# Retention and two feed-forward nets: the first two tiles' feature order, their first order of work, and the last copy

## The chip, the cores and the metric

The kernel runs on one core of one Trainium2 chip. The metric is the device time of an execution in microseconds; the median of the runs is compared. Engines: PE (TensorE, matrix products), DVE (VectorE), ACT (ScalarE), POOL (GpSimd) and SP (SyncE, which here only issues DMAs).

## The reference, cut to what matters

```python
# retention: B, H, S, D = 4, 8, 768, 64;  gamma per head
for t in range(S):
    state = gamma * state + outer(k[t], v[t])
    y[t] = q[t] @ state / sqrt(D)
x = y, as (3072 tokens, 512 features)
h = x @ w_in                                  # 512 x 2048
g = where(h >= 1, h, where(h <= -1, 0, (h + 1)**2 / 4))
x = g @ w_out                                 # 2048 x 512
out = ((x @ w1) * (x @ w2)) @ w3 @ w_out2     # 512 x 1024 twice, 1024 x 1024, 1024 x 512
```

## The kernel before, in words

The 768 steps are cut into six chunks of 128; chunk number c of all four batches makes token tile c with 512 tokens (B x C). Within a chunk retention is three products. "q" or "Q" words (function `scores`, line 507) make the 128 x 128 scores of each head from q and k; DVE multiplies them with a decay mask (line 520). "p" and "P" words (function `values`, line 562 in tiles 0 and 1, line 576 in tiles 2 to 5) make the output from the masked scores and v ("own" products) and, from tile 1 on, add the decayed queries times the state of the chunks before ("state queries", the operand `sbd`). "k" words (line 545) make keys times values, from which ACT and DVE make the next state. The output stands in PSUM, a tile of two banks, features on the partitions. `split_x` takes it out for tiles 0 and 1: ACT rounds it into xh (line 618), DVE takes the rest into xl (line 619); each product in full precision is made of three of such halves (lines 299 to 301). "h" words (tile 0) and "H" words (tile 1), function `plan_h`, are x @ w_in for one of 16 parts of 128 columns, 12 matmuls of 512 columns each; ACT (lines 658, 660) and DVE (line 661) make g of it.

The order of the 512 features differs: in tiles 0 and 1 partition 64h + d of block p holds feature d of head 2p + h; in tiles 2 to 5 the output of head 2p + h lies at partition half e, bank h, block j with p = j + 2e. So w_in's rows are needed in two orders. It is loaded from HBM in the first one by `load_win` (line 371), one DMA of 128 partitions for every 1024 words (pairs of 32-bit words, since the input is kept in its wide form), and converted to 32 bit by two ACT and four DVE operations (lines 332 to 345), then split into halves (lines 355, 357). For tiles 2 to 5 the converted w_in goes to a scratch tensor win_d and comes back in the second order by `load_permuted` (line 701): for each of eight units two DMAs of 64 partitions.

The order of PE's work at the start is written out in FIRST (line 43), where a digit is the batch (q, Q, p, P), the tile (k) or the part of w_in (h, H). A planner gives every other operation a due time from its consumers, loads among them, and a greedy emission writes all instruction streams; for PE it may take an operation from the next twelve if that can start sooner. PSUM has three tiles ("pe") for the scores, values and key products of tiles 0 and 1, and two banks for h and H. POOL scales the keys of tile 0, DVE those of tile 1 and the queries of tile 1 (line 536), once ACT has scaled the decay.

Behind that follow the products with w_out (y words; the chunks of tiles 2 to 5 run beside them), the first net for tiles 2 to 5 in pairs with seven instead of eight block products (`plan_hu`), the fold of w3 with w_out2, and the second net in the same way. The last tile's last 128 rows are copied out by `plan_out` in two halves, columns 0 to 255 by DVE with a DMA from SP, columns 256 to 511 by ACT with a DMA from ACT's queue (lines 931, 933, 1094).

Of the kernel before, what the change touches and what calls it, by code (L numbers as in the profile page):

```python
# [10 lines left out]
U32 = mybir.dt.uint32  # L11
# [5 lines left out]
C = 128  # L17
# [7 lines left out]
NP = H // 2  # L25
# [9 lines left out]
LEAD = 6.0  # L35
# [5 lines left out]
STAY = 8  # L41
MASKED = 6.8
FIRST = """
q0 q3 q2 q1 p2 p1 p3 p0 Q0 h0 Q2 Q1 h1 k0 P1 P2 Q3 P0 h2 P3 h3 H0 H1 H2 k1
h4 h5 H3 h6 h7 h8 H4 H5 H6 h9 H7 H8 h10 h11 h12 H9 h13 h14 H10 h15 H11 H12 H13 H14 H15
"""
KEYS = ("POOL", 1.2), ("DVE", 0.7), ("POOL", 1.2)
RATE = 360.0
# [202 lines left out]
def retention_then_two_ffns(  # L251
# [17 lines left out]
    nc = tc.nc  # L269
# [42 lines left out]
    def new_r(name):  # L312
        return work.tile([P, TT], F32, tag="r", name=name, bufs=3)

    plan = Plan({
# [3 lines left out]
    })  # L319
# [44 lines left out]
    win_d = [dram.tile([P, 1024], F32, name=f"win_d{n}") for n in range(NF1 // 2)]  # L364
    win_kept = {}

    def load_win(f, n):
        src = w_in[f // 2].bitcast(U32)
        c0 = f % 2 * 1024
        def fn(raw, j):  # L370
            nc.sync.dma_start(out=raw[:, 1024 * j:1024 * j + 1024], in_=src[:, c0 + 1024 * j:c0 + 1024 * j + 1024])
        return [(0.43, lambda raw, j=j: fn(raw, j)) for j in range(n)]

    def load_rows(*srcs):
        def one(j, src):
# [94 lines left out]
    def chunk(b, c):  # L470
# [42 lines left out]
        if c < 2:  # L513
            a = half(c, "a")
            a_at = lambda: a.ap.rearrange("p h (a t) -> p h a t", a=NP)
        else:
            a = Val("a", lambda: att.tile([P, 2, NP, C], F32, tag="a", name="a", bufs=1))
            a_at = lambda: a.ap
        if c < 2:
            plan.op("DVE", 1.25, lambda: nc.vector.tensor_tensor(  # L520
                out=a_at().rearrange("p h a t -> p (h a) t"),
# [3 lines left out]
        else:  # L525
            for h in range(2):
                plan.op("DVE", 0.7, lambda h=h: nc.vector.tensor_tensor(
                    out=a_at()[:, h], in0=ps_at(h).rearrange("p (a t) -> p a t", a=NP),
# [6 lines left out]
        if c:  # L535
            scaled_q = [plan.op(eng, many, lambda: ve.tensor_tensor(
                out=q_at(), in0=q_at(), in1=decay, op=ALU.mult), r=[decays], use=[q_], after=[qk, lq])]
# [13 lines left out]
        ps2 = new_ps(c)  # L551
        merged = c >= 2 and not last
        old = sbd.get(b)

        def values():
            q_t, v_t, a_t = q_at(), v_at(), a_at()
            if c < 2:
                for own in (True, False) if c else (True,):
                    for p in range(NP):
                        for h in range(2):  # L560
                            r = slice(64 * h, 64 * h + 64)
                            nc.tensor.matmul(
                                out=ps2.ap[64 * h:64 * h + 64, 0, p * C:(p + 1) * C],
                                lhsT=v_t[:, 2 * p + h, :] if own else old.ap[r, p, :],
                                rhs=a_t[:, h, p, :] if own else q_t[r, p, :],
                                start=p == 0 and own, stop=own == (c == 0), skip_group_check=True,
                            )
                return
            if merged:
                keys_values(ps2.ap[:, 0, 2 * C:2 * C + NP * D], True)  # L570
            for own in (True, False):
                for j in range(NP // 2):
                    for h in range(2):
                        for e in range(2):
                            p, r = j + 2 * e, slice(64 * h, 64 * h + 64)
                            nc.tensor.matmul(  # L576
                                out=ps2.ap[64 * e:64 * e + 64, h, j * C:(j + 1) * C],
                                lhsT=v_t[:, 2 * p + h, :] if own else old.ap[r, p, :],
                                rhs=a_t[:, h, p, :] if own else q_t[r, p, :],
                                start=own and j == 0 and not (merged and h == 0), stop=not own,  # L580
                                skip_group_check=True,
                            )

        pv_ops[b, c] = plan.op(
            "PE", 0.95 + (0.0, 0.86, 0.43)[min(c, 2)] + (0.43 if merged else 0.0), values,
            r=[a, old] if c else [a], w=[ps2], use=[v_, *([q_] if c else []), *([k_] if merged else [])],
            after=[lv, *scaled_q, *(scaled_k if merged else [])],
        )
# [1 line left out]
        if c >= 2:  # L590
            for kb in range(2):
                if (c, kb) not in xs:
                    xs[c, kb] = Val("w", lambda: wpool.tile([P, 2, 512], F32, tag="w", name="xs"))
                plan.op("ACT", 0.45, lambda kb=kb: nc.scalar.copy(
                    out=xs[c, kb].ap[:, :, b * C:b * C + C], in_=got()[:, :, kb]), r=[ps2], part=[xs[c, kb]])
        else:
            split_x(b, c, ps2, lambda: ps2.ap[:, 0, :].rearrange("p (a t) -> p a t", a=NP))

        def update(kv, at):

# [13 lines left out]

    def split_x(b, c, ps2, got):
        xh, xl = x_tile(c)
        view = lambda x: x.ap[:, :, b * C:b * C + C]
        hi = plan.op("ACT", 0.6, lambda: nc.scalar.copy(out=view(xh), in_=got()), r=[ps2], part=[xh])
        plan.op("DVE", 0.7, lambda: nc.vector.tensor_tensor(
            out=view(xl), in0=got(), in1=view(xh), op=ALU.subtract), r=[ps2], part=[xl], use=[xh], after=[hi])  # L620
# [66 lines left out]
    def keep_win(f, after):  # L687
# [5 lines left out]
            r=[w], w=[t], after=after)  # L693
        plan.op("POOL", 0.6, lambda: nc.gpsimd.dma_start(
            out=win_d[f // 2][:, 512 * (f % 2):512 * (f % 2) + 512], in_=t.ap), r=[t], w=[d], size=256)

    def load_permuted(u, n):

        of = win_d[n].rearrange("(h d) (i e w) -> e d i h w", h=2, i=2, e=2)
        for e in range(2):  # L700
            plan.op("SP", 0.45, lambda e=e: nc.sync.dma_start(
                out=u.ap[64 * e:64 * e + 64].rearrange("d (i h w) -> d i h w", i=2, h=2), in_=of[e]),
                r=[win_kept[2 * n], win_kept[2 * n + 1]], part=[u], size=400).lead = LEAD

    def load_whole(u, src, after):
        plan.op("SP", 0.45, lambda: nc.sync.dma_start(out=u.ap, in_=src), w=[u], size=512, after=after).lead = LEAD
# [101 lines left out]
    def plan_hu(i, n):  # L808
        if i < PAIR:
            u = Val("u", lambda: cpool.tile([P, 1024], F32, tag="u", name="u"))  # L810
            load_permuted(u, n)
            uh, ul = plan_unit(u)
            store_unit(n, (uh, ul))
        else:
            uh, ul = load_unit(n)
# [26 lines left out]
        def gate(f, src, src_at, second):  # L842
# [19 lines left out]
            out=c1.ap, in0=pair.ap[:, 0], in1=c1.ap, op=ALU.add), r=[pair], w=[c1])  # L862
# [9 lines left out]
            out=c2.ap, in0=pair.ap[:, 1], in1=c2.ap, op=ALU.add), r=[pair], w=[c2])  # L872
        gate(2 * n, c2, lambda: c2.ap, True)
        plan.op("DVE", 0.7, lambda: nc.vector.tensor_tensor(
            out=c3.ap, in0=c3.ap, in1=c5.ap, op=ALU.add), r=[c5], w=[c3])
# [193 lines left out]
    def plan_out(i, n, f, t):  # L1069

        p, w = pq[i, f, n], wc[f]
        if f == 0:
            evacs[i, n, t] = Val("acc", lambda: psum["acc"].tile([P, DM], F32, tag="acc", name="oacc"))
        ps = evacs[i, n, t]

        def fn():
            lh, ll = (p.ap[:, s, t * P:(t + 1) * P] for s in range(2))
            wh, wl = w.ap[:, 0, :], w.ap[:, 1, :]
            nc.tensor.matmul(out=ps.ap, lhsT=lh, rhs=wh, start=(f == 0), stop=False)  # L1079
            nc.tensor.matmul(out=ps.ap, lhsT=lh, rhs=wl, start=False, stop=False)  # L1080
            nc.tensor.matmul(out=ps.ap, lhsT=ll, rhs=wh, start=False, stop=(f == NF2 - 1))  # L1081

        out_ops[i, n, f, t] = plan.op("PE", 0.681, fn, r=[p, w], w=[ps])
        if f < NF2 - 1:
            return
        r0 = t * S + (2 * i + n) * C
        parts = [(t % 2, nc.sync, 0, 512)]
        if 2 * i + n == NTILE - 1 and t == 3:
            parts = [(0, nc.sync, 0, 256), (1, nc.scalar, 256, 512)]
        for eng, queue, c0, c1 in parts:  # L1090
            st = Val("st", lambda: new_st("ost"))
            plan.op("ACT" if eng else "DVE", 0.63, lambda eng=eng, c0=c0, c1=c1, st=st: evacuate(
                st.ap[:, c0:c1], ps.ap[:, c0:c1], eng), r=[ps], w=[st])
            plan.op("ACT" if queue is nc.scalar else "SP", 0.43, lambda queue=queue, c0=c0, c1=c1, st=st: queue.dma_start(
                out=out[r0:r0 + P, c0:c1], in_=st.ap[:, c0:c1]), r=[st], size=(c1 - c0) / 2).store = True

    with tc.manual_schedule():


        rows, zeros, ones, part = (  # L1100
            wpool.tile([P, 2, 512], F32, tag="w", name=name) for name in ("rows", "zeros", "ones", "part"))
        nc.sync.dma_start(out=small, in_=c_small)
        nc.vector.memset(rows[:, 0], 0.0)
        for h in range(2):
            r = slice(64 * h, 64 * h + 1)
# [6 lines left out]
        for h in range(2):  # L1112
            nc.vector.tensor_tensor(
                out=by_half(part, h), in0=causal.rearrange("p (o t) -> p o t", o=1).to_broadcast([P, NP, C]),
# [3 lines left out]
        for h in range(2):  # L1118
            ps = psum["e"].tile([P, 2, 512], F32, tag="pa", name="begin_ps")
            for n in range(BEGIN * (1 - h)):  # L1120
                nc.tensor.matmul(
                    out=ps[:, 1, 0:P], lhsT=zeros[:, 0, 0:P], rhs=zeros[:, 0, 0:P], start=True, stop=True)
            nc.tensor.matmul(
                out=ps[:, 0], lhsT=ones[:, 0, P * h:P * h + P], rhs=rows[:, 0], start=True, stop=True)
# [53 lines left out]
        qk, pv, kv, h = qk_ops, pv_ops, kv_ops, h_ops  # L1178
# [172 lines left out]
```

## Time and profile before

| | us |
|---|---|
| three runs: median (lowest to highest) | 997.19 (995.87 to 998.01) |
| the profiled execution, its own time | 994.71 |
| its span in the trace | 992.9 |
| PE busy in the span | 984.2 |
| DVE / ACT / POOL busy | 707.5 / 550.8 / 67.2 |

The span is what the trace covers of the profiled execution; the 1.8 us up to its own time lie around it. A page part gives busy shares in 40 slices of the span; the views by stretch give the same for chosen stretches; the timelines give single instructions (or merged runs of the same kind) with their start, their length and, in brackets, what the engine waited for just before. Matmul records overlap, since the engine is pipelined: what a block of them costs is read from start to start.

### The profile page before, as it was taken

What the parts mean: (1) busy time and instruction counts of PE and PEld (TensorE: products, weight loads), DVE (VectorE), ACT (ScalarE), POOL (GpSimd) and SP (SyncE); (2) the same over time, 40 slices, a digit from 0 to 9 for tenths busy, and PEclk for the clock granted to TensorE, in tenths of its full rate; (3) what the DMA queues carried; (4) which work ended last, traced back from release to release, by engine and by line L of the source; (5) the groups of instructions that cost most, each with busy time, mean ns of one, the idle gap of its engine ahead of it and who ended that gap; (6) DMA issues with size and microseconds to landing.
All of it is one profiled execution on the core that took longest, in us unless ns stands there. A gap on an engine that the chain in (4) does not pass through costs nothing.

```text
span 992.9 us, 15259 instructions
## 1 busy us (share of the span) xinstructions
PE 984.2 (99%) x5792; PEld 810.1 (82%) x5792; DVE 707.5 (71%) x1098; ACT 550.8 (55%) x971; POOL 67.2 (7%) x78
## 2 busy tenths in 40 slices
PE   8999999999999999999999999999999999999998
PEld 6888888878888888888888888888888888888886
DVE  8889888566577778776766788577874787657750
ACT  3778866343677767576766564444543446244430
POOL 1121244331000000000000000000000000000000
PEclk9999999999999999999999999999999999999999
DMA  9788899899988769899876971113131130301001
GB/s 326 290 275 307 295 354 382 306 336 360 352 273 284 277 220 403 325 340 341 322 284 252 391 285 68 43 43 106 54 115 40 47 117 33 117 32 43 22 21 65
DMA packets 71421, 212.10 MB, mean 214 GB/s; under 512 B 8370, under 2 KB 12850, under 8 KB 67380
## 3 DMA queue, kind: packets, MB, share of 16 engines
q1 hardware_dynamic: 66816, 195.79, 55.8%
q0 software_dynamic: 4384, 15.21, 3.9%
q8 instruction: 45, 0.74, 0.3%
q14 instruction: 28, 0.23, 0.1%
q10 hardware_dynamic: 148, 0.14, 0.0%
HBM read 154.48 MB, written 56.62 MB: 213 GB/s over the span
## 4 chain that ended last, share of the span: by engine, by line
PE 96%; DMA 2%; DVE 0%; ACT 0%; issue 0%; ACTq 0%; DVEq 0%
PE bank_a L1032 13%; PE y1acc L299 11%; PE y1acc L301 10%; PE y1acc L300 10%; PE bank L828 9%; PE bank_b L1032 7%; PE banks L828 7%; PE oacc L1080 4%; PE oacc L1081 4%; PE oacc L1079 4%; PE bank_c L1032 3%; PE hps L299 3%; PE hps L300 2%; PE hps L301 2%; PE pa L576 2%; PE qk_ps L507 1%
## 5 line engine op out<-in xcount | busy, mean ns | idle before, releaser
L299 PE MATMUL y1acc<-g,wo 128*128 128x512 f32 x384 | 151.4, 394 | 0.0
L301 PE MATMUL y1acc<-g,wo 128*128 128x512 f32 x384 | 149.7, 390 | 0.0
L300 PE MATMUL y1acc<-g,wo 128*128 128x512 f32 x384 | 149.6, 390 | 0.0
L1032 PE MATMUL bank_a<-yop,unit 128*128 128x512 f32 x576 | 145.7, 389 | 0.0
L1032 PEld LDWEIGHTS bank_a<-yop,unit 128*128 128x128 f32 x576 | 108.1, 188 | 22.5
L828 PE MATMUL bank<-xop,unit 128*128 128x512 f32 x384 | 95.3, 389 | 0.0
L299 PEld LDWEIGHTS y1acc<-g,wo 128*128 128x128 f32 x384 | 72.1, 188 | 17.7 <-issue 2.8
L301 PEld LDWEIGHTS y1acc<-g,wo 128*128 128x128 f32 x384 | 72.1, 188 | 15.5 <-DVE g L357 0.4
L828 PEld LDWEIGHTS bank<-xop,unit 128*128 128x128 f32 x384 | 72.0, 188 | 15.1 <-issue 0.2
L300 PEld LDWEIGHTS y1acc<-g,wo 128*128 128x128 f32 x384 | 72.1, 188 | 14.5
L1079 PE MATMUL oacc<-wc,p 128*128 128x512 f32 x192 | 74.7, 389 | 0.0
L1080 PE MATMUL oacc<-wc,p 128*128 128x512 f32 x192 | 74.7, 389 | 0.0
L1081 PE MATMUL oacc<-wc,p 128*128 128x512 f32 x192 | 74.7, 389 | 0.0
L1040 ACT COPY c<-bank_a 128x512 f32<-128x512 f32 x72 | 42.3, 588 | 56.0 <-PE bank_a L1032 55.5
L1032 PE MATMUL bank_b<-yop,unit 128*128 128x512 f32 x288 | 73.1, 389 | 0.0
L828 PE MATMUL banks<-xop,unit 128*128 128x512 f32 x288 | 73.1, 389 | 0.0
L1043 DVE TENSOR_TENSOR c<-c,c 128x512 f32<-128x512 f32 x48 | 33.2, 691 | 51.4 <-ACT c L1040 50.7
L715 ACT CAST unit<-unit_w 128x512 fp32r<-128x512 f32 x96 | 52.0, 565 | 30.0 <-DVE unit_w L723 25.5
L828 PEld LDWEIGHTS banks<-xop,unit 128*128 128x128 f32 x288 | 54.1, 188 | 11.2
L1032 PEld LDWEIGHTS bank_b<-yop,unit 128*128 128x128 f32 x288 | 54.1, 188 | 11.2
L717 DVE TENSOR_TENSOR unit<-unit_w,unit 128x512 fp32r<-128x512 f32 x96 | 57.5, 620 | 6.8 <-ACT unit L715 5.4
L355 ACT CAST p<-c 128x512 fp32r<-128x512 f32 x48 | 29.8, 621 | 48.0 <-DVE c L1043 48.0
(171 smaller groups left out, 1836.5 us busy)
## 6 DMA issues: line engine op xcount, KB each, us to landing
wo<-wo_d SPq DMA_DIRECT2D x80, 512.0 KB, 6.6
unit_w<-sp_wab SPq DMA_DIRECT2D x24, 512.0 KB, 3.3
raw<-in_w_in_dram SPq DMA_DIRECT2D x16, 512.0 KB, 6.6
wo_d<-wo POOLq DMA_DIRECT2D x16, 512.0 KB, 7.0
uh_d<-unit SPq DMA_DIRECT2D x8, 1024.0 KB, 4.7
raw<-in_w_dram SPq DMA_DIRECT2D x16, 512.0 KB, 7.8
unit<-uh_d SPq DMA_DIRECT2D x8, 1024.0 KB, 8.1
raw<-in_w3t_dram SPq DMA_DIRECT2D x8, 1024.0 KB, 6.7
```

What stands on the lines that cost most here:

```text
L299: nc.tensor.matmul(out=ps, lhsT=lh, rhs=rh, start=first, stop=False)
L300: nc.tensor.matmul(out=ps, lhsT=ll, rhs=rh, start=False, stop=False)
L301: nc.tensor.matmul(out=ps, lhsT=lh, rhs=rl, start=False, stop=last)
L715: plan.op("ACT", 0.18 + 0.00088 * (b - a), lambda: nc.scalar.copy(out=hi(), in_=u.ap[:, a:b]), r=[u], part=[v, done])
L717: plan.op("DVE", 0.15 + 0.00106 * (b - a), lambda: nc.vector.tensor_tensor(out=lo(), in0=u.ap[:, a:b], in1=hi(), op=ALU.subtract), r=[u, d ...
L828: nc.tensor.matmul(out=at[where](), lhsT=l, rhs=r, start=first and kb + k == 0, stop=kb == 1 and k == 2, skip_group_check=True,)
L1032: nc.tensor.matmul(out=vals[where].ap, lhsT=l, rhs=r, start=first and kb + k == 0, stop=kb == 1 and k == 2, skip_group_check=True,)
L1040: plan.op("ACT", 0.6, lambda: nc.scalar.copy(out=c.ap, in_=vals[where].ap), r=[vals[where]], w=[c])
L1043: plan.op("DVE", 0.7, lambda: nc.vector.tensor_tensor(out=c.ap, in0=x.ap, in1=y.ap, op=op), r=[v for v in (x, y) if v is not c], w=[c])
L1079: nc.tensor.matmul(out=ps.ap, lhsT=lh, rhs=wh, start=(f == 0), stop=False)
L1080: nc.tensor.matmul(out=ps.ap, lhsT=lh, rhs=wl, start=False, stop=False)
L1081: nc.tensor.matmul(out=ps.ap, lhsT=ll, rhs=wh, start=False, stop=(f == NF2 - 1))
```

## The change

Tiles 0 and 1 take the feature order of tiles 2 to 5. `values` loses its branch for c < 2: own products and state queries go over (j, h, e), the output into partition half e and bank h. `split_x` reads 256 columns from each of the two banks. `load_win` loads w_in in the second order at once: for a unit of n parts two DMAs, each into 64 partitions, with pieces of 512 words (2 KB); before, n DMAs of 128 partitions with 4 KB each. The first two units have n = 1, the other seven n = 2. What goes to win_d is then in the right order, and `load_permuted` gives way to one plain DMA of 512 KB for each of eight units. FIRST is written anew. The planner's cost of P falls from 1.81 to 1.38. The last copy is one of 512 columns by ACT with one DMA from SP.

```diff
 FIRST = """
-q0 q3 q2 q1 p2 p1 p3 p0 Q0 h0 Q2 Q1 h1 k0 P1 P2 Q3 P0 h2 P3 h3 H0 H1 H2 k1
-h4 h5 H3 h6 h7 h8 H4 H5 H6 h9 H7 H8 h10 h11 h12 H9 h13 h14 H10 h15 H11 H12 H13 H14 H15
+q1 q0 p0 q3 p1 p3 q2 p2 h0 h1 Q2 Q1 Q0 k0 P0 P1
+Q3 P2 h2 P3 H0 h3 H1 H2 k1 h4 H3 H4 h5 H5 h6 h7
+h8 H6 h9 H7 h10 h11 h12 h13 H8 H9 h14 H10 h15 H11 H12 H13
+H14 H15
 """
     def load_win(f, n):
-        src = w_in[f // 2].bitcast(U32)
         c0 = f % 2 * 1024
-        def fn(raw, j):
-            nc.sync.dma_start(out=raw[:, 1024 * j:1024 * j + 1024], in_=src[:, c0 + 1024 * j:c0 + 1024 * j + 1024])
-        return [(0.43, lambda raw, j=j: fn(raw, j)) for j in range(n)]
+        src = w_in[f // 2].bitcast(U32)[:, c0:c0 + 1024 * n].rearrange(
+            "(h d) (i e w) -> e d i h w", h=2, i=n, e=2)
+        def fn(raw, e):
+            nc.sync.dma_start(
+                out=raw[64 * e:64 * e + 64].rearrange("d (i h w) -> d i h w", i=n, h=2), in_=src[e])
+        return [(0.43, lambda raw, e=e: fn(raw, e)) for e in range(2)]
...
         def values():
             q_t, v_t, a_t = q_at(), v_at(), a_at()
-            if c < 2:
-                for own in (True, False) if c else (True,):
-                    for p in range(NP):
-                        for h in range(2):
-                            r = slice(64 * h, 64 * h + 64)
-                            nc.tensor.matmul(
-                                out=ps2.ap[64 * h:64 * h + 64, 0, p * C:(p + 1) * C],
-                                lhsT=v_t[:, 2 * p + h, :] if own else old.ap[r, p, :],
-                                rhs=a_t[:, h, p, :] if own else q_t[r, p, :],
-                                start=p == 0 and own, stop=own == (c == 0), skip_group_check=True,
-                            )
-                return
             if merged:
                 keys_values(ps2.ap[:, 0, 2 * C:2 * C + NP * D], True)
-            for own in (True, False):
+            for own in (True, False) if c else (True,):
                 for j in range(NP // 2):
                     for h in range(2):
                         for e in range(2):
...
-            "PE", 0.95 + (0.0, 0.86, 0.43)[min(c, 2)] + (0.43 if merged else 0.0), values,
+            "PE", 0.95 + (0.0, 0.43)[min(c, 1)] + (0.43 if merged else 0.0), values,
...
-            split_x(b, c, ps2, lambda: ps2.ap[:, 0, :].rearrange("p (a t) -> p a t", a=NP))
+            split_x(b, c, ps2, lambda: ps2.ap[:, :, 0:2 * C].rearrange("p h (a t) -> p h a t", a=2))
...
-        view = lambda x: x.ap[:, :, b * C:b * C + C]
+        view = lambda x: x.ap[:, :, b * C:b * C + C].rearrange("p (h a) t -> p h a t", h=2)
...
-    def load_permuted(u, n):
-        of = win_d[n].rearrange("(h d) (i e w) -> e d i h w", h=2, i=2, e=2)
-        for e in range(2):
-            plan.op("SP", 0.45, lambda e=e: nc.sync.dma_start(
-                out=u.ap[64 * e:64 * e + 64].rearrange("d (i h w) -> d i h w", i=2, h=2), in_=of[e]),
-                r=[win_kept[2 * n], win_kept[2 * n + 1]], part=[u], size=400).lead = LEAD
...
-            load_permuted(u, n)
+            plan.op("SP", 0.45, lambda: nc.sync.dma_start(out=u.ap, in_=win_d[n]),
+                    r=[win_kept[2 * n], win_kept[2 * n + 1]], w=[u], size=512).lead = LEAD
...
         if 2 * i + n == NTILE - 1 and t == 3:
-            parts = [(0, nc.sync, 0, 256), (1, nc.scalar, 256, 512)]
+            parts = [(1, nc.sync, 0, 512)]
```

## Rows read from the trace of the kernel before

**Rows 1.** The page: busy time and share by engine; granted clock in 40 slices.
```profile
PE 984.2 (99%) x5792; PEld 810.1 (82%) x5792; DVE 707.5 (71%) x1098; ACT 550.8 (55%) x971; POOL 67.2 (7%) x78
...
PEclk9999999999999999999999999999999999999999
```
**Rows 2.** Stretches: length, busy us by engine (instructions), clock, DMA share, GB/s.
```profile
6.00:12.00 6.00, 5.08 (x131) 3.65 (x129) 5.32 (x6) 0.24 (x1) 0.00 (x0) 1.00 1.02 348
12.00:18.00 6.00, 4.41 (x87) 4.23 (x91) 5.80 (x11) 4.74 (x9) 0.00 (x0) 1.00 1.05 399
...
20.00:35.00 15.00, 15.00 (x275) 12.62 (x273) 13.02 (x16) 10.69 (x20) 5.22 (x5) 1.00 1.05 382
35.00:100.00 65.00, 65.00 (x364) 52.72 (x360) 57.96 (x84) 52.75 (x90) 11.93 (x19) 1.00 0.80 275
...
150.00:300.00 150.00, 150.00 (x1486) 122.06 (x1481) 101.84 (x156) 78.92 (x166) 31.96 (x27) 1.00 0.97 334
```
**Rows 3.** Timeline of PE: start, length, line, operands, idle time before and releaser.
```profile
17.30 1.19 PE L507 MATMUL pe<-q,kT 64*64 64x128 f32 x32 [1.01 <-DMA kT<-in_kT_dram]
18.43 0.50 PE L299 MATMUL hps<-xh,win 128*128 128x512 f32 x1
...
21.37 1.10 PE L507 MATMUL pe<-qk 64*64 64x128 f32 x32
...
23.28 0.50 PE L299 MATMUL hps<-xh,win 128*128 128x512 f32 x1
...
26.27 2.09 PE L545 MATMUL pe<-vk 128*64 128x64 f32 x64
...
53.25 0.50 PE L299 MATMUL hps<-xh,win 128*128 128x512 f32 x1
```
**Rows 4.** Timeline of DVE, the same columns.
```profile
8.07 4.62 DVE L520 TENSOR_TENSOR a<-pe,mask 128x1024 f32<-128x1024 f32 x4 [0.37 <-PE pe L507]
...
17.34 0.68 DVE L619 TENSOR_TENSOR xl<-pe,xh 128x512 fp32r<-128x512 f32 x1
...
33.47 0.68 DVE L357 TENSOR_TENSOR win<-u,win 128x512 fp32r<-128x512 f32 x1
...
81.24 0.68 DVE L357 TENSOR_TENSOR win<-u,win 128x512 fp32r<-128x512 f32 x1
```
**Rows 5.** Timeline of PE: P1 and h2 (line 562), a chunk of tile 2 (line 576).
```profile
28.18 1.05 PE L562 MATMUL pe<-a,vk 128*64 128x128 f32 x16
29.16 1.09 PE L562 MATMUL pe<-q,sbd 64*64 64x128 f32 x16
30.18 1.09 PE L562 MATMUL pe<-a,vk 128*64 128x128 f32 x16
...
35.14 0.50 PE L299 MATMUL hps<-xh,win 128*128 128x512 f32 x1
...
133.34 0.67 PE L576 MATMUL pa<-q,sbd 64*64 64x128 f32 x16
133.83 1.05 PE L507 MATMUL qk_ps<-q,kT 64*64 64x128 f32 x32
```
**Rows 6.** Timeline of SP's queue: the issue of Q0's query load.
```profile
9.53 0.33 SPq L459 DMA_DIRECT2D q<-in_qT_dram  x1
```
**Rows 7.** DMA in 304.5 to 309.5 us, 40 slices, in GB/s: one permuted pair u<-win_d.
```profile
GB/s 33 33 0 0 0 0 0 0 0 0 0 0 0 0 0 0 0 41 66 57 139 262 352 377 352 344 213 205 221 262 238 238 238 197 148 156 74 66 8 8
```
**Rows 8.** Lines by form, 130 to 300 us: busy us, mean ns, idle us before.
```profile
L594 ACT COPY xs<-pa 128x256 f32<-128x256 f32 x32 | 10.8, 375 | 39.7 <-DVE sbd L607 21.6 <-PE pa L576 18.1
```
**Rows 9.** Timeline of the end: an earlier ACT copy, then the last copies and issues.
```profile
978.22 0.59 ACT L931 COPY ost<-oacc 128x512 f32<-128x512 f32 x1 [10.28 <-PE oacc L1081]
...
989.11 0.42 DVE L933 COPY ost<-oacc 128x256 f32<-128x256 f32 x1 [4.80 <-PE oacc L1081]
...
989.57 0.37 ACT L931 COPY ost<-oacc 128x256 f32<-128x256 f32 x1 [10.76 <-DVE ost L933]
989.97 0.38 ACTq L1094 DMA_DIRECT2D out_dram<-ost  x1
```

More of the change, by code (lines that the diff above doesn't have):

```diff
@@ L579, in values @@
                                 rhs=a_t[:, h, p, :] if own else q_t[r, p, :],
-                                start=own and j == 0 and not (merged and h == 0), stop=not own,
+                                start=own and j == 0 and not (merged and h == 0), stop=own == (c == 0),
                                 skip_group_check=True,
```

## The prediction

> **What bounds the kernel now.** I read the page's busy shares first: the matmul engine PE is busy 984.2 of 992.9 us and its granted clock is at the full level in every slice [rows 1]. So only two things can move the end: less PE work, or less time in which PE stands still. The stretches say where it stands still [rows 2]: PE is busy 15.00 of 15 us from 20 us on, 65.00 of 65 from 35 to 100, 150.00 of 150 from 150 to 300. The empty time lies in the first 18.4 us and behind the last matmul. From 150 on nothing can be won outside PE; whatever makes PE reach a later point earlier is kept, unless PE then outruns the other engines.
>
> The PE timeline of the start [rows 3] shows the end of the empty time: the scores of Q0 start at 17.30 after 1.01 us of waiting for their DMA, and h0 at 18.43 straight behind them. The DVE timeline [rows 4] shows what else holds h0: from the four masks at 8.07 (4.62 us) through the conversion of the first w_in unit to the last xl, which ends at 17.34 + 0.68 = 18.02, DVE hardly rests: it is busy 5.80 of the 6 us from 12 to 18 [rows 2]. DMA is the third full resource: 348 GB/s from 6 to 12 us, 399 to 18 and 382 from 20 to 35, its engines' share above 1.0 all that time [rows 2].
>
> **State queries in quarters.** In tiles 0 and 1 both the own products and the state queries of line 562 write halves in the order h; in tiles 2 to 5 (line 576) the queries already run in the order that the change gives to all. From start to start, a block of 16 records of state queries took 30.18 - 29.16 = 1.02 us on line 562 and 133.83 - 133.34 = 0.49 on line 576. The own products already ran both column halves side by side (29.16 - 28.18 = 0.98 for 16 records of full height), and go on so: 0 [rows 5]. Tile 0 has no state, tile 1 has four batches: 4 x 0.53 = **-2.1 us** of PE work, in a stretch where PE never waits (20 to 35 us), so all of it is on the path if nothing else takes over.
>
> **The new first order.** Before h2 both orders hold the same words (q0-3, p0-3, Q0-3, P0-2, h0, h1, k0); only their places change. What counts is Q0: it filled 17.30 to 18.43, while h0's operands were being finished. Now h0 and h1 come ahead of all Q. h0 needs DVE's ten us of work from 8.07 on, which the new order doesn't shorten, so it starts at about 18.1 instead of 18.43, and Q0's 0.95 us (Q2 and Q1 took 23.28 - 21.37 = 1.91 together [rows 3]) comes behind it: between 0 (the emission may look up to twelve operations ahead, and puts another Q into the hole) and +0.95. I take 0.95 - 0.33 = **+0.6**, the order as written.
>
> Then DVE is asked again. Before, Q0 stood ahead of h0 and Q2 and Q1 ahead of h1 [rows 3], so their masks ran while PE was in h0 and h1. Now the three Q end at 18.1 + 2.94 (h0) + 2.99 (h1) + 2.9 = 26.9, k0 (26.27 to 28.18, 1.9) ends at 28.8 [rows 3, 5], and P0 wants the mask of Q0, the third, and a scaled query (a 512-column operation like xl, 0.68 [rows 4]): with the first mask from 25.1, 3 x 1.2 + 0.7 gives 29.4. That is up to 0.6 us of waiting, or 0 if another P is taken first or DVE is quicker: **+0.3**. The conversion for h2 competes for the same DVE. Before, its low half of win ended at 33.47 + 0.68 = 34.15 for an h2 at 35.14 [rows 4, 5], so 1.0 us was spare, and DVE rested 15.00 - 13.02 = 2.0 us between 20 and 35 [rows 2]; together they cover the 0.7 us by which h2 now wants to start earlier.
>
> Later words: h5 to h8 move two places back (about 5.4 us each), h10 to h13 one or two forward. Part 12 of w_in was ready at 81.24 + 0.68 = 81.9 for a product fourteen places behind h4, at 53.25 + 14 x 2.73 = 91.5 [rows 3, 4], so a place or two forward costs nothing.
>
> **w_in by halves.** Sixteen loads of 512 KB, each 128 partitions, become pairs that write 64 partitions with 2 KB pieces; the first two units get two issues of 256 KB instead of one. SP has the room: it issued Q0's query at 9.53 in 0.33 us, and the tile was used at 17.30 [rows 3, 6], so two more issues are hidden by that lead; without it they would cost 0.7. What is not shown is the speed of such a load. Nearest below: the q, k and v loads (2 KB a partition, whole width) which fill the time from 6 to 12 us at 348 GB/s, and most of 12 to 18 at 399 [rows 2]: cost 0. Nearest above: the old permuted load of win_d, 64 partitions with 1 KB pieces, nearly alone on the engines: of its slices of 0.125 us sixteen stand above 100 GB/s, 2.0 us, and at the 240 of the later ones its 0.52 MB take 2.2, against 0.52 MB / 382 GB/s = 1.4 [rows 2, 7]. That is up to +0.8 for each 512 KB, 1.6 for the two units ahead of h1 and 3.2 with the unit of h2. But in those slices the first half (the nine up to 344 GB/s hold 0.25 MB) ran at up to 377 GB/s and only the second at about 240, and the pieces are half as long as the new ones; so I lean to the q loads, and little of it is on a path that DVE sets: **+0.2**, ends 0 and +3.2.
>
> A rule bears on that. The Trainium skill, page SBUF — State Buffer, section Door 1, says that 64 neighbouring partitions reach only 8 of 16 DMA ports, which would be half of its 436 GB/s. The slices at 352 and 377 GB/s, with only the first half under way, don't show that limit [rows 7]; with it each 512 KB would take about 2.4 us by an estimate from that page, beside the 2.2 of the third rival.
>
> **x split over two banks.** The new views read 2 x 256 columns from two banks instead of 512 from one. The copies of 2 x 128 columns from two banks took 375 ns, one of 256 from one bank 0.37 us [rows 8, 9], so nothing; a mask over both banks, 1024 columns, takes 1.2, not more than two operations of 0.68 [rows 4]. The removed permuted loads (16 become 8) lie between 200 and 340 us, where PE never waits (150.00 of 150 us [rows 2] in the first part of it): 0, and if that cover were gone, a gain of a few tenths.
>
> **The last copy.** Before: DVE copies 256 columns from 989.11 (0.42), ACT's half starts only at 989.57, though its column range is its own, takes 0.37, and its DMA is issued at 989.97 [rows 9]. After: ACT copies all 512 (0.59 on such a copy [rows 9]), to 989.70, and SP issues at about 989.74; 0.23 earlier, but with 256 KB in one queue instead of 128 KB in each of two. Ends -0.3 and +0.2, taken **-0.1**.
>
> **Sum.** -2.1 + 0.6 + 0.3 + 0.2 - 0.1 = -1.1 us. The profiled execution took 994.71 (span 992.9 and 1.8 around it) and would become 993.6. The median of the three runs is 997.19, 2.5 above that, and the runs spread over 2.1 us; the change is put onto the median: **996.1**.
>
> **Rivals.**
> 1. The whole gain. Another Q fills the hole ahead of h0 and DVE keeps up: -2.1 - 0.1 = -2.2, 995.0. For it: the same emission filled the hole with Q0 before. Against it: as written h0 and h1 stand first, and a Q can go ahead only if its data land by 17.2 again, as Q0's did, and the emission sees a wait at h0. Chance 0.20.
> 2. The gain moves into waits. DVE, full from 8 us on, sets h0 and then P0 and h2: the saved time is spent in waits of PE. Price: three masks, 3.6 us, that ran under h0 and h1, less the 2.0 us of DVE rests, are 1.6; -2.1 - 0.1 + 0.6 + 1.6 = 0.0, 997.2. For it: 5.80 busy us of 6 from 12 on. Against it: the conversion for h2 can fill DVE under h0 and h1 if its load comes early. Chance 0.18.
> 3. Slower: the half loads run at the pace of win_d's second half (240 GB/s). Mechanism: DMA is the full resource until 36 us, so 0.8 us for each of the four 512 KB ahead of h2 pushes the Q, k and v loads behind them; PE waits for k0 and Q0. Price +3.2, sum -2.1 - 0.1 + 0.6 + 0.3 + 3.2 = +1.9, 999.1. It decides from some 0.33 us for each 512 KB on (1.3 / 4), where the gain is gone. Chance 0.12.
>
> **How the numbers follow.** The forecast (995.3 to 996.8) has 0.50. A measurement of this kernel can tell about 0.2%, 2.0 us, from no change; with the runs' spread, the forecast gives 0.10 faster, 0.39 same, 0.01 slower; rival 1 0.13 and 0.07; rival 2 0.01, 0.15, 0.02; rival 3 0.05 same and 0.07 slower. Together faster 0.24, same 0.66, slower 0.10. The range reaches from 993.9 (rival 1 less a us of spread) to 998.9 (rival 2 plus spread and the better half of rival 3); about one in five stays outside.
>
> **What would show it.** In the profile after: line 576 alone with 16 state records in 0.49 us at tile 1; h0's first matmul near 18.1 with PE empty before it, and a Q behind h1; P0's wait for DVE under 0.7 us; w_in landings within the time of the q loads; h2 near 34.5 and P3 half a us shorter; nothing but PE from 35 to 988; the last DMA issued by SP 0.6 to 0.7 us behind the last matmul's end. Wrong would be: an h0 later than 19, PE waits for DMA between 20 and 36 us, or new waits between 60 and 110 us, where DVE and ACT are nine tenths busy.

## The result, and the profile after

| | before | after |
|---|---|---|
| four runs, median (lowest to highest), us | 996.79 (995.87 to 998.01) | 1011.19 (1009.04 to 1012.95) |
| ratio, 95% interval | | 1.0144 (1.0132 to 1.0156) |
| span of the profiled execution, us | 992.9 | 1009.4 |
| PE busy in it, us | 984.2 | 989.8 |

The change costs 14.4 us; 996.1 was forecast, and the range ended at 998.9. The page of the kernel after, its first line and its traffic in 40 slices of the span:

```profile
PE 989.8 (98%) x5792; PEld 810.5 (80%) x5792; DVE 704.1 (70%) x1097; ACT 549.5 (54%) x971; POOL 69.9 (7%) x78
...
GB/s 279 258 192 284 236 352 345 393 331 378 321 290 256 309 292 276 397 283 374 313 332 196 385 305 148 42 42 105 32 109 48 49 98 64 115 32 42 22 13 71
```

The stretches of the kernel after (columns as in [rows 2]):

```profile
10.00:20.00 10.00, 6.31 (x152) 5.07 (x144) 8.68 (x12) 5.70 (x9) 0.00 (x0) 1.00 1.05 297
20.00:30.00 10.00, 7.55 (x125) 5.86 (x126) 6.95 (x11) 2.80 (x5) 4.50 (x4) 0.97 1.07 285
30.00:40.00 10.00, 8.38 (x128) 6.79 (x129) 6.49 (x8) 5.55 (x12) 0.73 (x1) 0.86 1.02 266
40.00:50.00 10.00, 10.00 (x133) 7.80 (x132) 6.93 (x11) 6.65 (x13) 0.55 (x1) 1.00 1.06 279
50.00:60.00 10.00, 7.32 (x26) 5.37 (x25) 7.56 (x11) 6.14 (x10) 2.09 (x3) 0.84 0.49 155
...
80.00:90.00 10.00, 8.88 (x38) 6.68 (x36) 7.77 (x12) 8.35 (x17) 1.62 (x3) 1.00 0.94 256
90.00:100.00 10.00, 8.58 (x37) 6.80 (x38) 7.71 (x12) 7.63 (x13) 2.64 (x4) 1.00 1.05 292
...
150.00:300.00 150.00, 150.00 (x1613) 122.24 (x1610) 103.23 (x155) 75.25 (x165) 41.51 (x36) 1.00 0.92 342
```

From 10 to 40 us the 16 DMA engines are as full as before (1.02 to 1.07), but they move 266 to 297 GB/s instead of 382 to 399 [rows 2]. So they are still full from 40 to 50 us, where the rush was over in the kernel before:

```profile
40.00:50.00 10.00, 10.00 (x47) 8.18 (x44) 8.29 (x13) 7.50 (x11) 1.62 (x3) 1.00 0.45 139
```

DVE, which I took for the limit of the head, is less busy than before. PE, full from 20 us on before, is empty for 2.5 of the 10 us from 20, 1.6 of the next ten, 2.7 from 50 and 2.5 from 80 to 100. From 150 on PE is full as it was. The timeline of PE shows the same points of the work:

```profile
22.50 1.10 PE L512 MATMUL pe<-q,kT 64*64 64x128 f32 x32 [0.25 <-DMA kT<-in_kT_dram]
23.54 0.50 PE L301 MATMUL hps<-xh,win 128*128 128x512 f32 x1
...
28.63 1.26 PE L512 MATMUL pe<-q,kT 64*64 64x128 f32 x32 [2.07 <-DMA kT<-in_kT_dram]
30.41 0.63 PE L302 MATMUL hps<-xh,win 128*128 128x512 f32 x1
...
37.88 1.10 PE L512 MATMUL pe<-qk 64*64 64x128 f32 x32 [1.62 <-DVE q L541]
39.94 0.67 PE L569 MATMUL pe<-q,sbd 64*64 64x128 f32 x16
40.54 1.09 PE L569 MATMUL pe<-a,vk 128*64 128x128 f32 x16
43.78 0.50 PE L301 MATMUL hps<-xh,win 128*128 128x512 f32 x1
```

h0 starts at 23.54 instead of 18.43, h2 at 43.78 instead of 35.14 [rows 3, 5]. A Q waits 2.07 us for its k. The matmul at 30.41 takes 0.63 us where the same one takes 0.39 or 0.40 elsewhere: PE had stood still ahead of 28.63, and in 30 to 32 us its clock is granted at 0.50, the lower of its two levels (1.2 of 2.4 GHz):

```profile
30.00:32.00 2.00, 2.00 (x5) 1.61 (x6) 1.75 (x2) 0.00 (x0) 0.00 (x0) 0.50 1.15 170
```

PE's "busy" time is itself 5.6 us longer than before, with less work in it: the 384 matmuls of the h and H words take 4.4 us more, a part of them at the lower clock, and the four mask products at the start 1.6 more.

By the list of PE's waits the longest sum is not a wait for a DMA:

```profile
PE hps L301 <- DVE r L654: 5.4, 5, 2.7
```

Followed back, the longest of the five is one all the same. In ACT's stream a conversion of w_in (L334) stood until its half load had landed; the two steps that make g came behind it, DVE waited for ACT, and PE for DVE, which had to free the bank:

```profile
53.85 1.12 ACT L334 ACTIVATE u<-raw 128x1024 f32<-128x1024 f32 x1 [3.10 <-DMA raw<-in_w_in_dram]
...
56.16 0.69 DVE L654 SCALAR_TENSOR_TENSOR r<-hps,r 128x512 f32<-128x512 f32 x1 [2.10 <-ACT r L653]
...
56.90 0.79 PE L301 MATMUL hps<-xh,win 128*128 128x512 f32 x1 [2.68 <-DVE r L654]
```

And the loads into the tile raw, nearly all of w_in, by its line in the trace (landing after the issue, least, median, most), before and after:

```profile
DMA to landing us min/median/max: 4.9/6.6/7.9
```
```profile
DMA to landing us min/median/max: 5.6/7.9/11.5
```

### The profile page after: what moved, and what is told of

It is laid out like the page before. It is cut to its first block, busy times and chain, and to the rows that moved or that the text cites. A ratio compares the mean times of both kernels' runs of the same rounds, so it can differ in the third digit from the quotient of the medians.

```text
span 1009.4 us, 15233 instructions
## 1 busy us (share of the span) xinstructions
PE 989.8 (98%) x5792; PEld 810.5 (80%) x5792; DVE 704.1 (70%) x1097; ACT 549.5 (54%) x971; POOL 69.9 (7%) x78
## 4 chain that ended last, share of the span: by engine, by line
PE 89%; DMA 7%; ACT 2%; DVE 1%; issue 1%; SPq 1%; ACTq 0%; DVEq 0%
PE bank_a L1018 13%; PE y1acc L301 10%; PE y1acc L303 10%; PE y1acc L302 10%; PE bank L814 9%; PE bank_b L1018 6%; PE banks L814 6%; DMA raw<-in_w_in_dram 6%; PE oacc L1067 4%; PE oacc L1065 4%; PE oacc L1066 4%; PE bank_c L1018 3%; PE pa L569 2%; PE qk_ps L512 1%; DMA raw<-in_w_out_dram 1%; PE hps L301 1%
## 5 line engine op out<-in xcount | busy, mean ns | idle before, releaser
L814 PEld LDWEIGHTS banks<-xop,unit 128*128 128x128 f32 x288 | 54.1, 188 | 11.2
L1018 PEld LDWEIGHTS bank_b<-yop,unit 128*128 128x128 f32 x288 | 54.1, 188 | 11.2
L301 PE MATMUL hps<-xh,win 128*128 128x512 f32 x128 | 52.9, 413 | 5.5 <-DVE r L654 5.4
```

The costliest lines, as they stand in the source:

```text
L301: nc.tensor.matmul(out=ps, lhsT=lh, rhs=rh, start=first, stop=False)
L814: nc.tensor.matmul(out=at[where](), lhsT=l, rhs=r, start=first and kb + k == 0, stop=kb == 1 and k == 2, skip_group_check=True,)
L1018: nc.tensor.matmul(out=vals[where].ap, lhsT=l, rhs=r, start=first and kb + k == 0, stop=kb == 1 and k == 2, skip_group_check=True,)
```

## The experiments

Three theories. A: loads into 64 partitions move at about half the pace, and all that is lost comes from them. B: the new first order makes PE wait. C: the shorter pieces (2 KB) are what is slow. Every run below was compared with the kernel before on its own chip; ratios are to that.

**Taking the halves away, alone and with the order.**

e1_whole: w_in's rows permuted where its layout is made, so that the load is plain again.

```diff
-        src = w_in[...].rearrange("(h d) (i e w) -> e d i h w", h=2, i=n, e=2)
+        nc.sync.dma_start(out=raw[:, 1024 * j:1024 * j + 1024], in_=src[:, c0 + 1024 * j:...])   # n of these
-        "w_in": pairs(by_columns(inputs["moe_w_in"])),
+        "w_in": pairs(by_columns(w.reshape(2, 2, 2, D, FF1).transpose(2, 1, 0, 3, 4).reshape(DM, FF1))),
```

> The changed kernel, but w_in's rows are put into the new order where its layout is made ahead of the launch, so that each load is again one plain DMA of 128 partitions with 4 KB each; the quarters, the first order, the x split and the last copy stay. Theory A (loads into 64 partitions move at half the pace, and all that is lost comes from them): 993.5 to 996.5, w_in loads alone on the engines at 390 to 430 GB/s. Theory B (the new first order itself makes PE wait for DVE and DMA): 1004 to 1011. Theory C (the pieces of 2 KB are the slow part): as theory A.

e2_halves: the kernel before, w_in loads cut at partition 64.

```diff
+            nc.sync.dma_start(out=raw[64 * e:64 * e + 64], in_=src[64 * e:64 * e + 64])   # e = 0, 1
```

> The kernel before with one edit: each w_in load is cut at partition 64 into two DMAs, same rows, same place, pieces of 4 KB (8 KB for a unit of two parts); order, products and last copy as before. Theory A: the loads fall to about 220 GB/s and the kernel is slower by 4 to 14 us (1001 to 1011). Theory B and theory C: 996 to 998, since the order is the old one and no piece is short.

e3_old_first and e4_whole_old_first: the kernel after, and e1_whole, with the old FIRST.

```diff
-q1 q0 p0 q3 p1 p3 q2 p2 h0 h1 Q2 Q1 Q0 k0 P0 P1 ...
+q0 q3 q2 q1 p2 p1 p3 p0 Q0 h0 Q2 Q1 h1 k0 P1 P2 ...
```

> The changed kernel with the first order of the kernel before; the half loads stay. Theory A: 1006 to 1013, as the changed kernel. Theory B: 995 to 998. Theory C: as theory A.

> Whole w_in loads as in the first run of this set, and the first order of the kernel before: only the quarters, the x split and the last copy are left of the change. Theory A: 994 to 996 (2.1 us less PE work); the difference to the first run is what the new first order is worth without half loads, forecast 0 to 1 us to its disadvantage. Theory B: 994 to 996 too, with the first run 9 us or more above it.

| | w_in loads | first order | median, us | ratio (95%) |
|---|---|---|---|---|
| e1_whole | whole | new | 996.13 | 0.9990 (0.9976 to 1.0004) |
| e2_halves (all else as before) | cut at 64, 4 KB and up | old | 1009.41 | 1.0112 (1.0085 to 1.0138) |
| e3_old_first | halves, 2 KB | old | 1011.47 | 1.0144 (1.0111 to 1.0176) |
| e4_whole_old_first | whole | old | 999.54 | 1.0019 (1.0005 to 1.0032) |

Theory A holds in e1, e2 and e3. The cut alone, with the old order and long pieces, costs 11.2 us (8.5 to 13.8), and without the half loads the changed kernel is level with the one before. B falls with e3 (the old order mends nothing), C with e2 (its pieces are no shorter than before). Nor is the pace of the half loads set by the length of the pieces: with 8 KB pieces (e2, 60.2 to 63.2 us) it is 235 GB/s, with 2 KB (kernel after, 49 to 50.5 us) 227, each stretch with nothing but half loads in it:

```profile
DMA packets 102, 0.70 MB, mean 235 GB/s; under 512 B 16, under 2 KB 16, under 8 KB 16
```
```profile
DMA packets 173, 0.34 MB, mean 227 GB/s; under 512 B 7, under 2 KB 7, under 8 KB 173
```

The stretches of e1_whole show the head full again:

```profile
10.00:20.00 10.00, 7.02 (x153) 5.85 (x157) 9.29 (x15) 5.42 (x9) 0.00 (x0) 1.00 1.04 389
20.00:30.00 10.00, 10.00 (x166) 8.07 (x160) 9.86 (x13) 5.35 (x9) 5.67 (x5) 1.00 1.05 349
30.00:40.00 10.00, 10.00 (x166) 7.84 (x160) 8.92 (x12) 8.73 (x19) 0.55 (x1) 1.00 1.01 374
```

One thing missed: e4 was expected at 994 to 996 by both theories. It is 1.9 us slower than before with less PE work. Its PE waits more for DVE: by the list of PE's waits (total us, times, longest) 3.2 us for the release of a bank, where the kernel before has 0.3:

```profile
PE hps L299 <- DVE r L649: 3.2, 5, 1.3
```

**Which partitions?** e5_even_odd cuts the load, in the kernel before, into even and odd partitions: also 64 a DMA, also two issues.

```diff
+            nc.sync.dma_start(out=raw[e::2], in_=src[e::2])   # e = 0, 1
```

> The kernel before with each w_in load cut into two DMAs of 64 partitions, one for the even and one for the odd partitions, so that each DMA is spread over all 128. Against the cut at partition 64 (1009.4) only the set of partitions differs. Theory A1 (what is slow is a DMA into 64 neighbouring partitions, which reach half of the memory's DMA ports): 996 to 999, loads alone at 350 to 430 GB/s. Theory A2 (any DMA with 64 instead of 128 partitions is slow, by its number of rows or of issues): 1006 to 1011, loads at about 220 GB/s.

997.2 us, ratio 0.9997 (0.9982 to 1.0012): no cost. So it isn't the number of partitions nor of issues; only 64 neighbouring ones are slow. Nor is it the side that is read: the half loads of the kernel after read pieces of all 128 rows of w_in, those of e2 64 neighbouring rows, and both are slow. The DMA slices in GB/s of the kernel after from 48 to 60 us (0.3 us each; a pair of half loads of 512 KB goes until about 52, with the end of a store beside it until 49 and another store from 50.5 on), and the same pair of e5_even_odd from 49.1 to 52.3 us, with nothing else under way:

```profile
GB/s 239 205 239 225 246 218 225 218 218 205 246 218 314 219 184 55 335 396 191 14 0 0 0 0 0 0 0 0 0 0 0 0 0 55 341 369 314 410 423 396
```
```profile
DMA packets 156, 1.01 MB, mean 315 GB/s; under 512 B 32, under 2 KB 32, under 8 KB 34
```

The half loads stand at 205 to 246 GB/s for 3.6 us; even and odd partitions move 315 on the mean.

**Both halves at once.** e6_two_queues issues the upper half from ACT's queue; e9_paired does so for each part, both halves at the same point of the work.

```diff
-            nc.sync.dma_start(
+            (nc.scalar if e else nc.sync).dma_start(
                 out=raw[64 * e:64 * e + 64].rearrange("d (i h w) -> d i h w", i=n, h=2), in_=src[e])
```

> The changed kernel with the second half of every w_in load (partitions 64 to 127) issued from ACT's queue, so that both halves can be under way at the same time. Theory A1: the halves meet different ports and run side by side; most of the loss is gone, 996 to 1003, loads alone at over 330 GB/s. Theory A2: no more than 2 us better than the changed kernel, 1008 to 1012. ACT's 0.4 us for each of nine issues is in both.

> The changed kernel with every w_in load of one part issued as two halves at the same point of the work, partitions 0 to 63 from SP's queue and 64 to 127 from ACT's (in the run with two queues the planner had issued the halves up to ten us apart). Theory A1 (64 neighbouring partitions reach half of the ports): side by side the halves move at 340 to 430 GB/s; 996 to 1001, of which up to 2 us are for ACT's sixteen issues and its waits for a free buffer. If the halves stay at 220 GB/s even so: 1008 to 1013.

1014.35 us, 1.0167 (1.0145 to 1.0190), and 1016.23 us, 1.0187 (1.0164 to 1.0209): as a remedy both failed, against theory A1's expectation. The issues of e6_two_queues:

```profile
2.24 3.29 ACTq L375 DMA_DIRECT2D raw<-in_w_in_dram  x2
3.86 0.71 SPq L375 DMA_DIRECT2D raw<-in_w_in_dram  x1
13.55 0.61 SPq L375 DMA_DIRECT2D raw<-in_w_in_dram  x1
...
42.32 0.33 SPq L397 DMA_DIRECT2D win_d<-u  x1
42.75 0.62 SPq L375 DMA_DIRECT2D raw<-in_w_in_dram  x1
42.87 0.63 ACTq L375 DMA_DIRECT2D raw<-in_w_in_dram  x1
44.25 0.60 ACTq L375 DMA_DIRECT2D raw<-in_w_in_dram  x1
```

In the head the halves don't meet: ACT issues two upper halves at 2.24, the second lower one waits in SP's stream until 13.55, and the loads on ACT's queue go ahead of q and k. In e9_paired it is the same pair (2.24 and 13.66). Behind 42 us they do meet. The DMA views give the packets, MB and share of the engines by queue (q1 is SP's, q10 ACT's), here for 43.05 to 46.2 and for 47 to 48.4 us:

```profile
DMA packets 521, 1.21 MB, mean 386 GB/s; under 512 B 54, under 2 KB 54, under 8 KB 520
q1 hardware_dynamic: 520, 1.20, 102.0%
```
```profile
DMA packets 161, 0.31 MB, mean 218 GB/s; under 512 B 12, under 2 KB 12, under 8 KB 161
q10 hardware_dynamic: 85, 0.17, 56.8%
q1 hardware_dynamic: 76, 0.13, 47.5%
```

The 386 GB/s come from SP's queue alone: the loads and the store that it had issued ahead of its half, and at most the beginning of that half. Then a lower and an upper half are under way at once, and together they move 218 GB/s, no more than one half alone in the kernel after (227). So a second queue added no pace here. In e9_paired two such stretches moved 272 and 295 GB/s (49.1 to 51.1 and 82.7 to 84.2 us), more than one half alone and less than theory A1's 340 to 430. That neighbouring partitions are slow is shown by e5; why two halves of different partitions don't add up is open.

**Where the price is paid.** e10_early_halves and e11_late_halves cut, in the kernel before, only the first six parts, or only the other ten.

```diff
+        if f < 6:   # e11: f >= 6
+            return [(0.43, lambda raw, e=e: half(raw, e)) for e in range(2)]
```

> The kernel before with the loads of the first six of sixteen w_in parts (3 MB) cut at partition 64, the others whole. All loads cut gave +11 to +12 us. If the price is paid where DMA is the full resource (until about 36 us): 7 to 10 us slower than before, 1004 to 1007. If it is paid evenly: 4.5 us.

> The complement: parts 6 to 15 (5 MB) cut at partition 64, the first six whole. If the price is paid in the head: 0 to 3 us slower than before, 997 to 1000. If evenly: 7.5 us, 1004 to 1006.

1005.88 us, 1.0088 (1.0070 to 1.0106), and 998.26 us, 1.0020 (1.0003 to 1.0037). The first 3 MB cost 8.8 us, the other 5 MB 2.0; together 10.8, about the 11.2 of e2. The price lies where DMA is the full resource. By pace alone, 512 KB takes 0.52 MB / 227 GB/s = 2.3 us instead of 0.52 / 390 = 1.3: that is about 6 us for the first six loads, which cost 8.8, and about 10 for the other ten, which cost 2.0. What makes the rest of the 8.8 wasn't separated; a part is the clock, granted at 0.85 in 20 to 30 us of e10's trace, where it is 1.00 before:

```profile
20.00:30.00 10.00, 10.00 (x116) 7.57 (x111) 7.55 (x9) 4.57 (x10) 4.50 (x4) 0.85 0.96 261
```

**The rest of the change.** e12_new_first is the kernel before with the new FIRST alone.

```diff
-q0 q3 q2 q1 p2 p1 p3 p0 Q0 h0 Q2 Q1 h1 k0 P1 P2 ...
+q1 q0 p0 q3 p1 p3 q2 p2 h0 h1 Q2 Q1 Q0 k0 P0 P1 ...
```

> The kernel before with the new first order and nothing else: whole loads in the old feature order, halves for the state queries, the old last copy. With whole loads the new order came out 2.8 us better than the old one where the quarters were in. If the order has its own worth: 994 to 995.5 (2 to 3 us faster than before). If it only pays together with the quarters, or if my terms hold (+0.6 for the Q moved behind h0, +0.3 for DVE): 997 to 999.

998.61 us, 1.0011 (0.9998 to 1.0024): +1.1 us, as my two terms together (+0.9). So alone the order costs about one us, the quarters (with the x split and the last copy) under the old order cost two (e4), and all together gain one (e1). Of the three only e4 is clear of no change, but e1 and e4, which differ in the order alone, lie 3.4 us apart in their medians on one chip: with the quarters in, the new order is the better one.

**A better start.** In the trace of e1_whole the masks came late, so e7 (on e1_whole) and e8 (on the kernel before) let the two mask products use one row of K, which frees the small loads from a DVE fill.

```diff
-        nc.vector.memset(rows[:, 0], 0.0)
-        nc.vector.memset(ones[:, 0, 0:2 * P], 0.0)
-                lhsT=ones[:, 0, P * h:P * h + P], rhs=rows[:, 0], ...
+                lhsT=ones[64 * h:64 * h + 1, 0, P * h:P * h + P], rhs=rows[64 * h:64 * h + 1, 0], ...
```

> The changed kernel with whole w_in loads, and the start mended: the two mask products take one row of K (partition 0, then 64) instead of 128, so the clearing of rows and ones is not needed and the two small loads of decay rows leave at the start of ACT's stream instead of behind a DVE fill at 1.4 us. If the late mask products (1061 ns each against 592 in the trace of the kernel before) cost the head its time, the first mask is ready one to two us earlier and the kernel takes 993.5 to 995.5, 1 to 2 us under the run with whole loads alone; if DVE's order sets the head, no change, 995.5 to 997.

> The kernel before with the same mended start and nothing else, to see what it is worth there. If the mask products set the head: 995 to 996.5, 0.5 to 1.5 us faster than before; else as before.

996.78 us, 0.9997 (0.9986 to 1.0007), and 996.11 us, 0.9994 (0.9982 to 1.0005): no change, the other case of both expectations. The edits did what they were to do: the first masked scores start at 7.97 in e7 (8.78 in e1_whole) and at 6.56 in e8 (8.07 before). An earlier mask alone does not shorten the head. No version beat the kernel before by more than can be measured.

## Why the prediction was wrong, point by point

**w_in by halves: the step that failed.** I put +0.2 with an upper end of +3.2; it is +11.2 in the kernel before, and more in the changed one (1.0144 against 0.9990 without halves, 15 us). Two faults. First, the row. In [rows 7] I read the burst of the first 256 KB (up to 377 GB/s) as the pace of a half load and set the slices at about 240 behind it aside; the half loads of 512 KB stand at 205 to 246. The burst was no measure of the steady pace; what made it is open. With that I dismissed the rule of the Trainium skill, page SBUF — State Buffer, section Door 1, that 64 neighbouring partitions reach 8 of 16 ports. By an estimate from the Trainium skill's figure there, half of 436 GB/s is 218, and the 227 and 235 GB/s of these traces agree with it. By the Trainium skill's formula in that section even or odd partitions would reach all ports; the 315 GB/s and the time of e5 agree with that. Second, the price. I counted 0.8 us for each of the four 512 KB ahead of h2 as the upper end, and put them nearly all off PE's path. It was 1.0 each, and what hangs on it is more than its own time: on one shared queue q, k and v wait behind the halves, PE stands (2.07 us for one k), and comes back at the lower clock. Rival 3 named this mechanism and its sign; its chance of 0.12 and its 999.1 were too low.

**State queries: right in kind, too large.** From start to start a block takes 40.54 - 39.94 = 0.60 where own products follow; the 0.49 of [rows 5] was in front of scores. In front of own products it was 1.02 before, so the saving is 0.42 and 4 x 0.42 = 1.7 us, not 2.1. I compared two blocks with different neighbours.

**The new first order: the sum right by luck, the steps not.** Forecast +0.9, measured alone +1.1 (interval -0.2 to +2.4). But h0 did not come at 18.1 with PE empty before it. In e1_whole a Q stood ahead of it, as rival 1 had it, and h0 came at 21.20:

```profile
20.21 1.05 PE L509 MATMUL pe<-q,kT 64*64 64x128 f32 x32
21.20 0.50 PE L301 MATMUL hps<-xh,win 128*128 128x512 f32 x1
...
36.08 0.50 PE L301 MATMUL hps<-xh,win 128*128 128x512 f32 x1
```

I had missed that p0 now stands right behind q0 and must wait for the mask of its own scores, by the list of waits of e1_whole:

```profile
PE pe L566 <- DVE a L522: 3.4, 3, 1.6
```

and that DVE takes parts of the conversion for h1 ahead of the last xl (the lines of DVE in e1_whole, where the last xl is the one at 20.12):

```profile
18.58 0.43 DVE L342 TENSOR_SCALAR u<-u 128x512 uint32<-128x512 uint32 x1
...
19.52 0.68 DVE L345 CUSTOM_DVE_ANT_0 u<-raw,u 128x1024 uint16<-128x1024 uint16 x1
20.12 0.69 DVE L609 TENSOR_TENSOR xl<-pe,xh 128x512 fp32r<-128x512 f32 x1
```

h2 of e1_whole is at 36.08, 0.9 behind [rows 5] where I had 0.7 ahead.

**Later words, x split, win_d:** as forecast, nothing. PE of e1_whole is full from 20 to 70 us; xl of two banks takes 0.68 or 0.69, as in [rows 4]; from 150 to 300 us its PE is busy 150.00 of 150.

**The last copy:** forecast -0.1. From the start of the first copy to the end of the span it is 992.9 - 989.11 = 3.8 before [rows 9] and 1009.4 - 1005.61 = 3.8 after: 0.

```profile
1005.61 0.59 ACT L917 COPY ost<-oacc 128x512 f32<-128x512 f32 x1 [10.29 <-PE oacc L1067]
1006.23 0.33 SPq L1080 DMA_DIRECT2D out_dram<-ost  x1
```

Without the half loads the sum of my terms was -1.1 - 0.2 = -1.3; e1_whole measured -1.0 (interval -2.4 to +0.4). That much of the forecast stands, though partly because errors of opposite sign met.

## What to carry to other kernels

The price of a slower load depends on where it stands: the same cut cost 8.8 us on the first 3 MB, where the DMA engines were full and q, k and v came behind it, and 2.0 on the other 5 MB. So where the DMA engines are full, a new shape of load is the first term to settle, from a transfer long enough to show a steady rate, and not the last. Cutting a tile into its lower and upper 64 partitions about halved the pace here; a cut into even and odd partitions cost nothing, and a permutation that is known ahead belongs into the layout of the data. A new order and the work that it orders can't be judged one by one: here the quarters alone came out 1.9 us slower and the order alone no better, both together a little faster, if at all.

## What the runs showed of the hardware that was not expected

The share of the DMA engines says nothing about the pace: in e6_two_queues it is 1.02 at 386 GB/s and 1.04, both queues together, at 218, where two half loads into different 64 partitions come from two queues.

The four records of the mask products took 592 to 767 ns before, and 1027 to 1190 after, though the granted clock stands at 1.00 in the first 10 us of both. PE had waited 0.38 us ahead of them before and 0.88 after. Line L1123 before and L1109 after (least, median, most):

```profile
L1123 PE MATMUL begin_ps<-rows,ones x4: 592/592/767, 4.9 to 6.4; 128*128 128x512 f32 x4
```
```profile
L1109 PE MATMUL begin_ps<-rows,ones x4: 1027/1057/1190, 5.4 to 8.1; 128*128 128x512 f32 x4
```

What made them longer is open. The longer form stood in part or all of the records in most other executions too (median 1061 in e2 and e4, 842 in e1), not in the profiled one of the kernel before, at 994.71 the shortest of those first shown. That it owes its time to these records isn't shown: e12 has a median of 592 too, and took 997.74.
